# A fused attention and expert-layer kernel: wide code weights, paired evictions, another order of score products, another order table

## The chip, the cores and the metric

The kernel runs on one core of one Trainium2 chip. The metric is the device time of one execution in microseconds. Three runs of the kernel before gave 787.03, 787.33 and 788.19 us; their median, 787.33 us, is the time before.

## The reference

Sixteen heads (2 batches of 8) of 768 tokens and 64 dimensions go through an attention in which a token sees only those keys that fall into its bucket; the result goes through two expert layers without a gate.

```python
q_bits = (einsum('bhsd,dk->bhsk', q, proj) > 0)     # 6 bits a token; k_bits likewise
q_bucket = sum(q_bits * 2 ** arange(6))             # 64 buckets
mask = q_bucket[:, :, :, None] == k_bucket[:, :, None, :]
scores = where(mask, q @ k.T / 8, -1e9)
attn = exp(scores - max); attn = attn / (attn.sum() + 1e-9)
x = (attn @ v) as [1536, 512]
h = x @ w_in;  g = h where h >= 1, 0 where h <= -1, else (h + 1) ** 2 / 4
x = g @ w_out                                       # w_in 512x2048, w_out 2048x512
out = ((x @ w_a) * (x @ w_b)) @ w_out2              # w_a, w_b 512x1536, w_out2 1536x512
```

## The kernel before

Nearly every float32 product is made of three products of an f32r high and low part (high x high, high x low, low x high). A product here is one TensorE matmul of 128 rows, mostly with 384 moving columns (512 in the last layer, 64 or 65 in pv).

**Attention.** For each head, `tk` transposes k (and `kh`, `kl` hold its high and low part), `tq` transposes q into `qt`. `signs` multiplies both with the projection into a bank `kp`, and ScalarE turns that into sign bits `bit` (f16, 103 rows: four groups of six bits, 32 rows apart, with a row of ones). `buckets` multiplies the bits with a constant table of codes: for each of 64 buckets it yields a number whose sign tells whether a token is in that bucket. This goes into a bank `kid`, from where `same` (L588 on ScalarE, L590 on VectorE) writes the upper half of `kl` as 0 or 1, and `f` writes `q2`, which holds a large penalty and the low part of q. So a score tile is four products: `qt` x `kh` and `q2` x `kl`, once for each of the two halves of the keys; each half has a bank of its own (`qk`, L675). A row minimum on VectorE (`mn`, L679) and an exponential on ScalarE (`sm`, L681) follow, then a high and a low part in f16 (`phi`, `plo`), their transposes by DMA on SyncE's queue (`pth`, `ptl`), and the products `pv` with v (L748).

`buckets` has three forms. In batch 0, `i` of 0 or 1 (16 banks, `both`): a product `low` x `qt` (L615) that copies q's low part into rows 64 to 127 of the bank, and then a product of the bits with 64 columns of the code (L616) on top of rows 0 to 63; `f` reads the bank (L621 and L622 on ScalarE, or L624 on VectorE). In batch 0, `i` of 2 (8 banks): a product of 128 code columns (L581), and two reads by `same`, one for each half of the keys. In batch 1 (16 banks): a product of 128 code columns (L581), one read by `same` from rows 64 to 127 and one by `f` (L608 on ScalarE, L610 on VectorE) from rows 0 to 63.

**Expert layers.** `hp` (L1046) is x @ w_in, `acc` (L1258) is g @ w_out; weights come in as 512 KB blocks (`words`), are joined from two 32-bit words and split into high and low parts. The second layer (L1179, L1284) forms x @ w_a and x @ w_b by a seven-product scheme. The first hp needs the attention of all eight heads of the first 384 tokens; from there on attention and expert work are interleaved, and behind the last pv, at some 366 us, there are only expert layers.

**The order.** `Program.add` collects some 3500 operations with the engines that may do each, and its dependencies. Their order, and the engine of each, stands in the table ORDER (L34): a letter for the engine (p TensorE, v VectorE, a ScalarE, g GpSimd, s SyncE's DMA queue) and the step to the operation's number. `schedule` (L225) reads it; each engine works through its own operations in this order. The numbers that `add` gets with an engine are a planner's costs and do nothing at run time; `after` is a dependency that only the order has to respect. Which buffer of a kind an operation gets is set by the order too: `issue` (L241) hands out the one that came free first. Banks of kind `p` (2 of them) and `px` (2, batch 0's early part) hold kid, kp, tk, tq, pv and hp in turn.

Of the kernel before, what the change touches and what calls it, by code (L numbers as in the profile page):

```python
# [39 lines left out]
v-14 a p24 a s-8 v-3 a v142 a-145 v7 g10 v172 p-170 v g18 p-17 v2 a-1 p-8 v g3 p24 a v p-5 a-56 g2 a55 v70 p-102  # L40
p19 v163 g-160 v11 a-25 v12 a182 p-158 a a24 a-53 v54 v-94 v41 a4 p18 s159 s-200 p48 a p-21 v14 v-13 g-2 a18
a221 s-227 g p36 a v p-5 a v p-25 v g-7 g9 a-10 p17 a2 a-1 s-36 a27 s197 a p-192 v p30 v65 p-88 s-40 p31 v33 p2
a-29 g-7 a14 v-3 g2 g15 p-3 v170 v-221 s49 a s-26 a14 g19 v165 a-159 v-11 g-62 p102 a v p-5 a v a-38 p212 p-201
v g11 p-5 a2 s-48 p33 s3 a26 g-20 v v12 p-11 a3 g16 p14 v s-48 v80 g a-66 p7 p27 a67 v a-106 a17 v-5 v-44 v190
s-168 p28 v a20 p15 v g-86 a44 g21 a g12 s-18 v a26 p-25 v p20 v148 s-185 a38 a-20 s97 g-80 p-6 v v-25 p54 a v
a-30 p25 a s-56 g51 a g12 p-16 v a p-15 v150 p-112 a s s-43 a73 g v-15 p-30 a6 s448 a p-438 v-21 p19 v-14 a p123
v-193 s40 p35 a9 p8 p-2 a-1 a33 v-22 v94 v v-109 v7 p26 a-25 g-6 v32 v3 v g-19 s-33 a19 a-4 p15 v p22 a-17 p6 v
s-42 p36 a110 a-93 p9 g-18 a-13 a14 v24 s25 v-24 g-13 v6 s-30 p21 a-11 p42 a5 g v-36 a5 a26 v-49 a19 a12 v-30
p26 p28 a s-59 p27 v-33 v37 v2 g13 p-3 v p25 v s50 a v a-61 v p27 v-26 s-39 v99 a-91 a13 p19 v s-12 a48 v-11
a-41 p22 v v19 a-23 s-43 p25 g17 v7 s-27 a19 v11 p26 v g-2 p6 a p a-37 a79 a-47 s-57 p30 g28 a5 g42 p-27 v-47 v  # L50
v47 a-20 p-15 a v p51 v s23 a v v s-97 a53 a4 s9 a v-13 g-74 p40 a v47 v a-47 v g15 a38 a-52 g p14 a s-39 p57 a
s-4 v20 v7 a-76 s126 g-125 a34 a19 a73 p-61 v p15 a v-47 v v60 a-29 g11 v49 v-73 v-17 p19 p-1 p38 v s-45 a34 s19
a p-46 v27 g13 s-21 p-4 v a v54 p-22 p-15 p-33 s37 p4 s-22 v27 a3 v-2 a-20 g s83 a-57 a28 g v-30 a-19 p16 v s6
p-15 p13 v p-16 v34 a-53 v s68 p-47 a9 a25 p a a-20 g a52 v-15 s-22 p-4 v a v40 v p-53 a p37 a s-116 a79 v35 g20
v-60 a83 g a-51 p-3 s-12 p18 v a v-4 v-28 a p40 a g p-6 a s35 v-44 v-108 p130 v p-27 p-3 p38 g-58 p21 v21 v17 a6
g a-29 v a17 p a-5 a-33 p42 v a-4 v-38 s34 g10 a v18 s-5 a-5 s-18 v19 a-11 v23 p3 a v a-4 a-43 p25 p32 p-21 a22
p-31 s24 v-14 p-13 a14 v-7 p29 a p-35 g-25 p65 p6 v-24 p29 a-15 v13 v-2 g-29 s-4 p48 a-36 v v v-5 v a28 s-19 a15
a11 s-44 a61 p-23 p-24 a34 v-3 a4 s-22 v12 v11 p-24 a-32 v88 s-29 g-18 s7 v-20 p v43 a-51 p42 v a-18 g22 g-16
a-18 v v s140 a-103 g21 s-12 p-13 v s25 p-21 p-44 a45 a-15 v v-14 v10 v5 g-4 a13 p29 a19 a-43 p10 a s19 a-5 g-24
a25 p-11 v p-13 a50 v-26 g27 s-81 a44 a-10 p-3 p9 v s66 p-78 v6 v p-4 s15 p106 a-104 v-162 g p175 a v-14 p22 p2  # L60
a80 v a-107 p25 a-18 p50 v a-37 p-4 v p100 a v a-110 v p16 p20 v-35 g11 a-4 p17 v-16 a165 v s-158 a34 p-49 s40
g-45 p56 s-24 a5 g v-9 s151 a-140 a v v-11 s2 p24 v-97 g a134 v a-66 p22 a p11 v p4 a-63 a37 a-9 v36 v-15 p26
g-37 p59 a-82 v v a43 a-20 v v v19 a a14 p-47 a a84 p-61 a24 s-23 a18 g43 p-49 v p59 a p-28 p-47 p46 a-30 v10 a
v33 v-39 v-4 p59 g-54 p22 s-15 a118 a-105 a35 s-59 p39 v a-55 a58 v-33 s27 v-12 v-39 v a98 s-84 p14 a a-4 a203
# [1335 lines left out]
```

## Time and profile before

| what | us |
|---|---|
| median of three runs | 787.33 |
| the profiled execution | 789.12 |
| its span, first to last instruction | 787.3 |
| TensorE busy | 755.8 (96%) |
| VectorE busy | 665.3 (85%) |
| ScalarE busy | 488.9 (62%) |
| GpSimd busy | 381.7 (48%) |

The profiled execution is not one of the three runs. Busy time is an average over stages with different limits, so it says little here of what a stage is worth. A product of 384 columns stands in the timeline with 0.33 us, but its end is modelled; products overlap, and what one costs is read from the distance of the starts, 0.17 us in a dense stretch. For the same reason TensorE's idle time before a product is some 0.16 us shorter than what the wait costs.

### The profile page before, as it was taken

How to read it: one execution, taken by the hardware profiler on the slowest of the kernel's cores; microseconds unless marked ns; L12 is line 12 of the kernel's file. 1: busy time of each engine (PE TensorE's matmuls, PEld its weight loads, DVE VectorE, ACT ScalarE, POOL GpSimd, SP SyncE). 2: the span in 40 equal slices, each digit the busy share in tenths (PEclk: the TensorE clock that was granted, in tenths of full speed). 3: DMA queues.
4: the chain of work that ended last, by engine and by line, in shares of the span. 5: the costliest groups of instructions: out<-in, count | busy, mean ns of one | idle time of the engine just before them, and what ended most of it. 6: DMA issues, size and time to landing. Idle time of an engine off the chain costs nothing.

```text
span 787.3 us, 14720 instructions
## 1 busy us (share of the span) xinstructions
PE 755.8 (96%) x5532; PEld 696.1 (88%) x5532; DVE 665.3 (85%) x1171; ACT 488.9 (62%) x896; POOL 381.7 (48%) x336
## 2 busy tenths in 40 slices
PE   7888799999999999899999999999999999999998
PEld 4677699998988989889999999999999889999986
DVE  6899899999888998878876856799989897898775
ACT  5889889999988877676554454454434754243232
POOL 1777546546585677563153224354534107534430
PEclk9999999999999999999999999999999999999999
DMA  7999999999799778664012331014432002322011
GB/s 217 194 197 211 234 235 248 235 222 224 165 182 167 133 145 156 122 97 92 2 54 90 102 103 55 27 54 134 134 108 80 14 1 76 99 70 92 1 41 40
DMA packets 202792, 95.50 MB, mean 121 GB/s; under 512 B 165217, under 2 KB 197217, under 8 KB 202721
## 3 DMA queue, kind: packets, MB, share of 16 engines
q1 hardware_dynamic: 202272, 94.39, 52.9%
q8 instruction: 43, 0.70, 0.4%
q14 instruction: 29, 0.23, 0.1%
q10 hardware_dynamic: 448, 0.17, 0.1%
HBM read 53.65 MB, written 3.15 MB: 72 GB/s over the span
## 4 chain that ended last, share of the span: by engine, by line
PE 77%; DVE 11%; ACT 6%; DMA 3%; issue 2%; POOL 1%; SPq 0%; ACTq 0%; POOLq 0%; DVEq 0%
PE hp L1046 15%; PE acc L1258 14%; PE acc L1284 12%; PE mx L1179 12%; PE mz L1179 6%; PE s L675 6%; PE pv L748 5%; PE acc L1179 3%; DVE mn L679 2%; ACT sm L681 2%; PE kp L563 1%; DMA kn<-in_k 1%; PE tq L530 1%; DVE F L948 1%; PE tk L490 1%
## 5 line engine op out<-in xcount | busy, mean ns | idle before, releaser
L376 POOL TENSOR_TENSOR plo<-sm,phi 128x768 f16<-128x768 f32 x58 | 100.7, 1740 | 40.8 <-ACT phi L371 25.7
L679 DVE TENSOR_REDUCE mn<-s 128x1 f32<-128x768 f32 x96 | 91.3, 953 | 15.8 <-PE s L675 15.2
L681 ACT ACTIVATE sm<-s,mn 128x768 f32<-128x768 f32 x96 | 86.3, 900 | 26.2 <-DVE mn L679 25.1
L675 PE MATMUL s<-kh,qt 128*128 128x384 f32 x192 | 70.5, 367 | 4.4 <-ACT sm L681 4.2
L376 POOL TENSOR_TENSOR wlo<-F,whi 128x512 fp32r<-128x512 f32 x41 | 57.0, 1393 | 34.5 <-ACT whi L371 24.1
L1232 ACT ACTIVATE t<-hp,half 128x384 f32<-128x384 f32 x64 | 37.1, 580 | 58.4 <-PE hp L1046 54.4
L675 PE MATMUL s<-kl,q 128*128 128x384 f32 x192 | 65.5, 341 | 2.1 <-ACT q L622 1.0
L376 POOL TENSOR_TENSOR gl<-t,gh 128x384 fp32r<-128x384 f32 x31 | 36.1, 1166 | 49.0 <-ACT gh L371 31.8
L1284 PE MATMUL acc<-whi,gl 128*128 128x512 f32 x144 | 56.7, 394 | 0.0
L1284 PE MATMUL acc<-wlo,gh 128*128 128x512 f32 x144 | 56.7, 393 | 0.0
L1284 PE MATMUL acc<-whi,gh 128*128 128x512 f32 x144 | 56.0, 389 | 0.0
L748 PE MATMUL pv<-vc,pth 128*128 128x65 f16 (+1 forms) x1152 | 51.9, 195 | 2.7 <-DVE q L610 1.7
L1046 PE MATMUL hp<-xsh,whi 128*128 128x384 f32 x152 | 52.0, 342 | 1.6 <-DVE q L610 0.8
L371 ACT ACTIVATE phi<-sm 128x768 f16<-128x768 f32 x63 | 52.8, 841 | 0.7
L1258 PE MATMUL acc<-gh,whi 128*128 128x384 f32 x144 | 52.9, 367 | 0.0
L1241 DVE SCALAR_TENSOR_TENSOR t<-t,hp 128x384 f32<-128x384 f32 x64 | 35.1, 549 | 19.7 <-ACT t L1237 15.8
L748 PEld LDWEIGHTS <-pth 128*128 128x128 f16 x1152 | 42.7, 99 | 9.8 <-issue 9.6
L1046 PE MATMUL hp<-xsh,wlo 128*128 128x384 f32 x152 | 50.9, 335 | 0.0
L1046 PE MATMUL hp<-xsl,whi 128*128 128x384 f32 x152 | 50.9, 335 | 0.0
L1258 PE MATMUL acc<-gh,wlo 128*128 128x384 f32 x144 | 48.5, 337 | 0.0
L1258 PE MATMUL acc<-gl,whi 128*128 128x384 f32 x144 | 48.4, 336 | 0.0
L942 ACT ACTIVATE wab<-stage 128x512 f32<-128x512 f32 x55 | 36.2, 665 | 17.5 <-DMA stage<-in_moe_w_b 3.9
(253 smaller groups left out, 2538.4 us busy)
## 6 DMA issues: line engine op xcount, KB each, us to landing
stage<-in_moe_w_out SPq DMA_DIRECT2D x31, 512.0 KB, 3.9
stage<-in_moe_w_b SPq DMA_DIRECT2D x17, 512.0 KB, 3.7
stage<-in_moe_w_a SPq DMA_DIRECT2D x17, 512.0 KB, 3.6
stage<-in_moe_w_in SPq DMA_DIRECT2D x16, 512.0 KB, 4.7
kn<-in_k SPq DMA_DIRECT2D x16, 192.0 KB, 4.1
out<-ob SPq DMA_DIRECT2D x12, 256.0 KB, 2.1
vn<-in_v SPq DMA_DIRECT2D x4, 384.0 KB, 5.2
vscan<-in_v SPq DMA_DIRECT2D x4, 384.0 KB, 4.8
```

Of the source, the lines that this page charges most:

```text
L371: nc.scalar.activation(dst, src, ACTF.Copy)
L376: (nc.vector if e == "dve" else nc.gpsimd).tensor_tensor(dst, a, b, ALU.subtract)
L675: nc.tensor.matmul(s()[:, i, 0:HC], x()[:, qs], t[i]()[:, 0:HC], start=(n == 0), stop=(n == 1))
L679: add({"dve": c_dve(S)}, lambda e: nc.vector.tensor_reduce(mn(), s()[:, :, 0:HC], AX.XY, ALU.min), r=[s], w=[mn])
L681: o = add({"act": c_act(S, True) + 0.093}, lambda e: nc.scalar.activation(sm().rearrange("p (c n) -> p c n", c=2), s()[:, :, 0:HC], ACTF.E ...
L748: nc.tensor.matmul(o[:, t, 0:D + 1 - i], w()[:, t, c, :], vcs[t]()[:, c, (1 - i) * D:(2 - i) * D + 1 - i], start=(n == 0), stop=(n == 3 * ...
L942: add({"act": 0.556}, lambda e: nc.scalar.activation(ab(), t()[:, :, :, 1].bitcast(F32), ACTF.Prelu, scale=SHIFT, alpha=SIGN), r=[t], w=[a ...
L1046: nc.tensor.matmul(o()[:, 0:TB], a()[:, kk, :], m(), start=(n == 0), stop=(n == 3 * KD - 1))
L1179: nc.tensor.matmul(view()[:, 0:TB], a()[:, sl], m(), start=(start and n == 0), stop=(n == 5), skip_group_check=not start)
L1232: add({"act": 0.465}, lambda e: nc.scalar.activation(t(), o()[:, 0:TB], ACTF.Relu, bias=half, scale=0.5), r=[o], w=[t])
L1258: nc.tensor.matmul(ac()[:, 0:TB], a()[:, d, :], x(), start=(f == 0 and n == 0), stop=(f == F1 - 1 and n == 2))
L1284: nc.tensor.matmul(ac(), a()[:, ts], x().rearrange("p k n -> p (k n)"), start=(f == 0 and n == 0), stop=(f == F2 - 1 and n == 2))
```

## The change

- `qk`: the loops over the half of the keys and over the two terms are swapped, so the four products of a score tile run kh of bank 0, kh of bank 1, kl of bank 0, kl of bank 1.
- `both`: the bits' product comes first, and it takes 128 code columns, of which 64 are zeros, instead of 64; the low part is accumulated on it.
- The code table is 576 columns in nine blocks of 64 instead of 384 columns in three pairs, two blocks being zeros, so that every bits' product takes two neighbouring blocks. For `i` of 2 the two halves of the bank change places.
- `buckets`: of the two reads of a bank the second names the first in `after`.
- ORDER is another table of the same length; the change moves operations on every engine and between engines.

```diff
--- before.py
+++ after.py
@@ -32,128 +32,128 @@
 ORDER = """
-s s2 v3 v p12 a2 v-19 p9 s18 s4 v-28 p3 p8 a-4 v a-4 v p12 s-18 v42 p-29 g30 v-17 p-12 a5 p3 v8 v-6 a-1 p-3 v
-p-5 s276 a v s-284 g p33 a v p a v p-13 v s-10 a p28 a s-26 a v s25 a-20 s12 a31 p-29 v v242 s-23 p-213 p2 s328
...
-a-11 v p11 p7 p-1 v5 v-15 v16 p-4 p7 p-1 p-1 v-4 v a6 v a-15 v p17 v v p-4 p11 a s p-8 a p-5 p7 a s-2 s3
+s3 v3 v p12 a2 s-20 v v3 p6 a v p-5 a v s286 a p-281 p6 a p-6 p v280 s-265 v266 s-270 a p-6 s-20 v42 v v-22 p a
+a p-8 v14 s-20 g p33 p3 a-2 p-9 a12 v-2 s-15 a p24 a p-5 v-3 p10 v-22 a g17 v-2 a g11 p-4 s-34 v v5 p a26 p8 a a
...
+v5 v g-16 p11 p p6 p a v-13 a6 v g7 p-4 p5 v3 v p-2 p9 a s p-8 v s p-6 p7 a s
@@ -345,7 +345,7 @@
     zq_h = const.tile([128, 135], F32R, name="zq_h")
     zq_l = const.tile([128, 135], F32R, name="zq_l")
     zk = const.tile([128, 135], F32R, name="zk")
-    code = const.tile([128, 3, 128], F16, name="code")
+    code = const.tile([128, 576], F16, name="code")
     least = cst[:, 129:130]
     times = cst[:, 130:131]
     thr = cst[0:NR, 128:129]
@@ -578,9 +578,10 @@
         up, dn = slice(0, 64), slice(64, 128)
 
         def mm(e):
-            nc.tensor.matmul(s()[:, 0:HC], code[0:NR, i], bit(), start=True, stop=True)
-
-        def same(c, x):
+            at = 64 * (1 if i == 2 else 3 - 3 * i if b else 5 + 2 * i)
+            nc.tensor.matmul(s()[:, 0:HC], code[0:NR, at:at + 128], bit(), start=True, stop=b > 0 or i == 2)
+
+        def same(c, x, after=()):
             o = d["kl"][c]
 
             def g(e):
@@ -588,11 +589,10 @@
                     nc.scalar.activation(o()[up, 0:HC], s()[x, 0:HC], ACTF.Sign, scale=-1.0)
                 else:
                     nc.vector.tensor_scalar(o()[up, 0:HC], s()[x, 0:HC], 0.0, None, ALU.is_lt)
-            add({"act": c_act(HC, True), "dve": c_dve(HC)}, g, r=[s], w=[o])
+            return add({"act": c_act(HC, True), "dve": c_dve(HC)}, g, r=[s], w=[o], after=after)
         if i == 2:
             add({"pe": 0.18}, mm, r=[bit], w=[s])
-            same(0, up)
-            same(1, dn)
+            same(0, dn, [same(1, up)])
             return
         qt, o = d["q"][c], Buf("q2", [128, HC], F32R)
         d["q2"][c] = o
@@ -601,19 +601,19 @@
             add({"act": c_act(HC), "dve": c_dve(HC, True), "pool": c_pool(HC)},
                 lambda e: copy_on(e, o()[dn], qt()[dn]), r=[qt], w=al[1:])
             add({"pe": 0.18}, mm, r=[bit], w=[s])
-            same(c, dn)
+            first = same(c, dn)
 
             def f(e):
                 if e == "act":
                     nc.scalar.activation(o()[up], s()[up, 0:HC], ACTF.Relu, scale=PEN)
                 else:
                     nc.vector.tensor_scalar(o()[up], s()[up, 0:HC], 0.0, PEN, ALU.max, ALU.mult)
-            add({"act": c_act(HC, True), "dve": c_dve(HC)}, f, r=[s], w=al[:1])
+            add({"act": c_act(HC, True), "dve": c_dve(HC)}, f, r=[s], w=al[:1], after=[first])
             return
 
         def both(e):
-            nc.tensor.matmul(s()[:, 0:HC], low, qt(), start=True, stop=True)
-            nc.tensor.matmul(s()[up, 0:HC], code[0:NR, i, up], bit(), start=False, stop=True, skip_group_check=True)
+            mm(e)
+            nc.tensor.matmul(s()[:, 0:HC], low, qt(), start=False, stop=True)
         add({"pe": 0.35}, both, r=[bit, qt], w=[s] + al)
 
         def f(e):
@@ -670,8 +670,8 @@
 
         def mm(e):
             qs = slice(jj * 128, (jj + 1) * 128)
-            for i in range(2):
-                for n, (x, t) in enumerate(((qt, kh), (q2, kl))):
+            for n, (x, t) in enumerate(((qt, kh), (q2, kl))):
+                for i in range(2):
                     nc.tensor.matmul(s()[:, i, 0:HC], x()[:, qs], t[i]()[:, 0:HC],
                                      start=(n == 0), stop=(n == 1))
         add({"pe": 0.8 if b else 0.86}, mm, r=[qt, (q2, 0), (q2, 1)] + [t[i] for t in (kh, kl) for i in range(2)], w=[s],
@@ -1348,7 +1348,7 @@
         nc.scalar.dma_start(out=cst, in_=consts)
         for i in range(2):
             nc.scalar.dma_start(out=prj[i * D:(i + 1) * D], in_=proj)
-        nc.scalar.dma_start(out=code.rearrange("p i n -> p (i n)"), in_=codes)
+        nc.scalar.dma_start(out=code, in_=codes)
         nc.vector.tensor_copy(idr, idt)
         pr.issue()
 
@@ -1369,11 +1369,12 @@
     c[0:64, 130] = PEN
     bits = np.zeros((32, 64), dtype=np.float16)
     bits[0:nb, 0:64] = 2 * (np.arange(64) >> np.arange(nb)[:, None] & 1) - 1
-    g = np.zeros((128, 3, 128), dtype=np.float16)
-    for i, at, part in ((0, 0, 0), (0, 64, 2), (1, 0, 1), (1, 64, 3), (2, 0, 2), (2, 64, 3)):
-        g[32 * part:32 * part + 32, i, at:at + 64] = bits
-        g[32 * part + nb, i, at:at + 64] = -nb if part > 1 else 1 - nb
-    g = g.reshape(128, 384)
+    g = np.zeros((128, 9, 64), dtype=np.float16)
+    for i, part in enumerate((1, 3, 2, 0, 2, 0, None, 1)):
+        if part is not None:
+            g[32 * part:32 * part + 32, i] = bits
+            g[32 * part + nb, i] = -nb if part > 1 else 1 - nb
+    g = g.reshape(128, 576)
     return c, g
```

## Rows read from the trace of the kernel before

**Rows 1.** Windows: us, busy us (instructions) by engine, clock, DMA share, GB/s.
```profile
10.00:97.00 87.00, 70.99 (x719) 56.55 (x718) 78.05 (x130) 73.82 (x130) 56.86 (x48) 0.96 1.03 209
97.00:160.00 63.00, 63.00 (x565) 59.21 (x566) 60.78 (x100) 56.71 (x104) 33.88 (x29) 1.00 1.06 239
160.00:260.00 100.00, 95.98 (x950) 88.01 (x949) 87.83 (x144) 87.73 (x157) 59.48 (x48) 1.00 0.94 190
260.00:380.00 120.00, 115.33 (x1114) 107.89 (x1111) 102.46 (x169) 85.39 (x146) 73.04 (x61) 1.00 0.64 116
380.00:788.00 408.00, 402.57 (x2166) 380.84 (x2164) 330.76 (x612) 181.83 (x356) 157.63 (x146) 1.00 0.21 66
```

**Rows 2.** TensorE's timeline, 287 us: start us, us, engine, line, operation, tiles.
```profile
287.49 0.34 PE L1258 MATMUL acc<-gh,wlo 128*128 128x384 f32 x1
287.67 0.34 PE L581 MATMUL kid<-bit,code 103*128 103x384 f16 x1
287.71 0.48 PE L675 MATMUL s<-kh,qt 128*128 128x384 f32 x1
288.03 0.34 PE L675 MATMUL s<-kl,q 128*128 128x384 f32 x1
288.20 0.33 PE L675 MATMUL s<-kh,qt 128*128 128x384 f32 x1
288.37 0.34 PE L675 MATMUL s<-kl,q 128*128 128x384 f32 x1
```

**Rows 3.** Chain that ended last, pieces: start us, us, what.
```profile
96.82 3.22 PE hp L1046 x17
```

**Rows 4.** Timeline of TensorE at 111 us.
```profile
111.47 0.34 PE L615 MATMUL kid<-qt,eye 128*128 128x384 f32 x1
111.74 0.35 PE L616 MATMUL kid<-bit,code 103*64 103x384 f16 x1
112.02 0.44 PE L1258 MATMUL acc<-gh,whi 128*128 128x384 f32 x1
...
112.47 0.35 PE L1258 MATMUL acc<-gh,wlo 128*128 128x384 f32 x1
```

**Rows 5.** Timeline of TensorE at 147 us.
```profile
146.86 0.42 PE L615 MATMUL kid<-qt,eye 128*128 128x384 f32 x1
147.21 0.35 PE L616 MATMUL kid<-bit,code 103*64 103x384 f16 x1
...
147.95 0.34 PE L1258 MATMUL acc<-gh,wlo 128*128 128x384 f32 x1
```

**Rows 6.** Lines L616, L581: weight loads, ns min/median/max.
```profile
L616 PEld LDWEIGHTS <-code x16: 106/106/106, 10.2 to 157.7; 103*64 103x64 f16 x16
...
L581 PEld LDWEIGHTS <-code x24: 95/98/100, 9.5 to 336.1; 103*128 103x128 f16 x24
```

**Rows 7.** TensorE's waits, 0 to 97 us: total us, times, longest.
```profile
PE kid L616 <- ACT bit L568: 0.6, 1, 0.6
```

**Rows 8.** Page, costliest groups: busy us, mean ns; idle us.
```profile
L748 PEld LDWEIGHTS <-pth 128*128 128x128 f16 x1152 | 42.7, 99 | 9.8 <-issue 9.6
```

**Rows 9.** Waits of ScalarE and VectorE, 97 to 380 us: total us, times, longest.
```profile
ACT kl L588 <- DVE q L610: 3.2, 2, 2.0
...
DVE q L610 <- ACT kl L588: 3.4, 3, 1.7
```

**Rows 10.** TensorE's waits, 97 to 380 us.
```profile
PE pv L748 <- DVE q L610: 1.7, 2, 0.9
PE s L675 <- DVE kl L590: 0.9, 1, 0.9
...
PE hp L1046 <- DVE q L610: 0.8, 1, 0.8
```

**Rows 11.** Line L610: duration in ns min/median/max.
```profile
L610 DVE TENSOR_SCALAR q<-kid x9: 509/548/550, 175.4 to 310.3; 64x384 fp32r<-64x384 f32 x9
```

**Rows 12.** GpSimd's groups, 0 to 97 us: busy us, mean ns; idle us.
```profile
L373 POOL CAST phi<-sm 128x768 f16<-128x768 f32 x7 | 6.5, 924 | 7.8 <-ACT sm L681 7.8
```

More of the change, by code (lines that the diff above doesn't have):

```diff
@@ L40 @@
[L40 to L64, printed above, removed]
@@ new lines @@
+g13 v-6 g2 v141 v-187 a51 g14 a-16 g19 g10 a199 p-174 a a78 v-46 v-1 p-73 p11 a p8 v-19 v42 a-22 a v194 v-233
+p55 v p-26 v s-4 v26 g s-33 v117 a-119 a15 p v104 a-103 p-12 a8 a154 p-143 p25 a v-12 g-11 v-2 v57 v86 g-85 s-80
+v19 p22 v a-15 a-4 g22 s-6 a129 p-120 a s-24 g19 g13 a-17 p-12 a15 g-23 g40 p4 v v p-4 a p-9 v a v-27 v p69 a
+p-16 a v81 p-92 p13 a-9 s62 p-59 a v-7 a s-50 p35 s40 v-15 s-28 p154 s-153 p45 v-21 p19 s-11 a40 v-43 v17 a36
+g-64 g13 s2 a-3 g43 p-38 s92 v27 v-71 a-49 a15 s17 a-22 p8 a v-5 a6 p-4 v71 v34 g-90 s2 p12 a-32 g21 a34 g v-52
@@ new lines @@
+p11 v18 p5 a v-2 v-21 s124 g-110 a-13 a14 g12 p-16 v p-6 v p25 v a-20 g17 g7 p-13 a41 p-31 p21 a5 v-35 a v-18
+v27 a p11 s-19 a10 v18 p6 a p-32 p37 p5 a52 v-59 s-9 v-9 a a25 p p18 s-64 v38 a49 v10 v-76 a55 g a-53 v-56 p57
+v73 s-76 a21 v-3 g2 g7 v16 v v22 v-41 a-6 a11 p26 v p4 a44 s-104 p30 g28 a-33 a32 v4 p a s30 a s-67 v4 v p12
+v-37 v38 v a38 p13 v p-20 v a v15 v p-49 g12 v22 s40 a-73 a74 s-94 a21 v-16 g-24 g96 s24 s-47 a21 p-4 v a g-67
+p32 a21 v-37 s109 a-108 p34 a p20 v17 v a-57 v21 v14 s-19 p44 a s8 s-26 a-42 a92 v-108 v55 v-38 a v91 p-46 g-6
@@ new lines @@
+g-83 g8 s s a-12 v58 g-45 g17 g-108 p83 a p80 a-50 s366 a-290 a-32 a-29 v36 v p-81 v p6 v v v36 v29 p-56 a-16
+a22 g16 s2 a-23 p v p49 a v p69 g-35 p-76 a p112 a-121 g-106 p226 a-110 p-6 p114 v-113 v7 p3 a-12 a3 v10 a v29
+p39 a v p-57 v a-10 s-7 s5 a17 s5 g6 v41 a a27 p-84 v a p126 a a p-97 a g-77 p48 g-2 v82 v-27 p100 p2 a-5 v-149
+a g4 a21 a40 v59 p-119 g-4 s2 v146 p-128 v p6 a p123 p-2 a-25 v p-84 s-8 v32 v-60 v61 a-44 v139 a-126 v83 g-95
+v9 g-84 g171 p-90 v a a11 a14 p107 s-129 p130 p-128 a v23 v-6 v108 a-107 p111 p-115 v s19 p94 v-127 a115 a-100
@@ new lines @@
+g20 v-3 p85 a p-82 a83 s-85 g13 g-46 v115 a-79 v83 p-91 v p-11 a a a10 g17 s5 g-1 v69 v v7 g p a a p-110 v v
+p114 p p-96 v a g9 p a v77 v p7 a g p-3 a-4 p-88 v a s3 v7 v75 a-74 s5 a209 p-131 g-79 s2 v70 a19 a-11 p-88 v a
+p99 a-8 a-82 v89 p-2 v-9 v a p-86 v g88 v-2 a-85 v13 a82 p-6 g-75 p-9 p83 s-61 g-1 s2 a68 a-90 p4 v p79 p18 a-96
+g17 a71 v-3 v v-161 v162 a7 a3 p-86 p7 v-6 a86 v a-86 a8 s4 g70 p-3 p-1 v-96 v94 v-69 v4 s2 p84 a a p-22 p14
+a-85 v109 v v-133 p97 v9 v11 g-10 p13 v p-10 v11 a-18 g p4 p p16 v v p-102 a92 p17 g-16 g-118 a111 g a-86 p96 v
```

193 lines of the change are left out of this document (99 added, 94 removed).

## The prediction

> **What bounds the kernel now.** I read the windows by stage first. From 380 us to the end TensorE is busy 402.57 of 408 us [rows 1]. That is more than half of the span, and no order of the work can shorten it: products of 384 columns follow each other every 0.17 us there, as from 288.03 to 288.37 in [rows 2]. From 97 to 160 us TensorE is busy all the time too [rows 1]. What can move is TensorE's idle time before 97 us (87.00 - 70.99 = 16.0 us between 10 and 97) and between 160 and 380 us (4.0 + 4.7 = 8.7 us), and what a product costs beyond 0.17 us. Before 97 us there is only attention to run, for the first product of the expert layers (hp) starts at 96.82 [rows 3]; VectorE is busy 78 and ScalarE 74 of 87 us there, the DMA share is 1.03, and the granted clock is 0.96 on average [rows 1]. That stage is a mesh of limits, and a saving on TensorE reaches the end only in part. Behind 97 us the expert layers fill TensorE, and what one of its products or waits costs there comes off the end in full.
>
> **The bits' product: what is removed.** Sixteen banks (`both`, batch 0) get a low-part product (L615), and on top of it the bits' product whose f16 weights are 64 columns wide (L616). In [rows 4] the pair starts at 111.47, two more products follow from 112.02 on, and the next starts at 112.47: 1.00 us for four products. In [rows 2] the 128-column bits' product (L581) stands between f32r products: from 287.49 to 288.20 four products start, the bits' one among them, 0.71 us. The 64-column form thus costs 1.00 - 0.71 = 0.29 us more than the 128-column one with f32r work on both sides, which is how it will stand after the change (bits, then low part). Where a transpose or a pv product stands ahead, as at 147 us, the four take 147.95 - 146.86 = 1.09 us [rows 5], 0.38 more than 0.71. The interval from L615 to L616 tells the two forms apart (0.27 as in [rows 4], 0.35 or more as in [rows 5]). Behind 97 us there are five such banks, three of the first and two of the second form: 3 x 0.29 + 2 x 0.38 = 1.6 us, all on the path. Before 97 us there are eleven, four of the first form and seven of the second: 4 x 0.29 + 7 x 0.38 = 3.8 us, of which I count half, 1.9 us (bounds 0 and 3.8), since TensorE waits in that stage for engines that are not shortened.
>
> The wider weights are no cost by the trace: the load of 103x128 takes 98 ns, that of 103x64 106 ns [rows 6]. The Trainium skill ("TensorE: Matmul & The Clock Gate", LDWEIGHTS) speaks against this edit: a load's time goes with its column count, P / 1.2 ns. By that rule 64 more columns are 53 ns, 16 x 53 ns = 0.9 us lost, and the sum would end at 781.4 instead of 780.5 us. The trace disagrees, 98 against 106 ns, so the measurement decides.
>
> **Bits first.** The wait for the bits now stands ahead of both products, where the low part used to run before it; everything on TensorE's queue is behind it. One wait of this kind is to be seen before 97 us, 0.6 us [rows 7], and it would grow by one product, 0.17 us. If each of the sixteen waited it would be 16 x 0.17 = 2.8 us; I take nothing for the one, as it lies in the half that I don't count.
>
> **Scores alternate their banks.** The four products of a score tile stay; only kl of bank 0 and kh of bank 1 change places. In [rows 2] 288.03 to 288.20 changes the bank, 288.20 to 288.37 does not, and both steps are 0.17 us: no gain and no loss. The row minimum waits for all four either way. Equal weights now stand side by side; the pv products already use each pth block twice in a row, and a load is still issued for each of the 1152 [rows 8]. The bound on the gain is 0.173 - 0.160 us (384 columns at 2.4 GHz) for 192 products, 2.5 us; I take 0. A wait for kl or q2 now finds two products ahead of it instead of one, 0.17 us less a time; one such wait is in [rows 10] (s for L590), and I leave it out.
>
> **Two evictions in succession.** A bucket bank is read twice, for kl and for q2. When the two reads are on different engines they don't overlap in the trace, they wait for each other: between 97 and 380 us ScalarE stands 3.2 us for VectorE's q2, VectorE 3.4 us for ScalarE's kl [rows 9]. The program keeps them apart already, so the new `after` adds no wait on the chip; it makes the order table follow it. By the new table 15 of the 16 such banks of batch 1 have both reads on one engine, by the old one 5; of batch 0's eight pairs of kl, 7 against 3. TensorE's waits that end with such a read (L610, L590) sum to 1.7 + 0.9 + 0.8 = 3.4 us behind 97 us [rows 10]. I take two thirds, 2.3 us (bounds 0 and 3.4): a bank's second read, 0.5 us [rows 11], still has to end before pv or hp can have the bank. The Trainium skill ("PSUM — Partial Sum Buffer", PSUM bank collisions) says that two engines may read different quadrants of one bank at once, and kl's and q2's reads do lie in different ones; by that rule succession would give up an overlap of 0.5 us in each of 16 banks, and this term could be a loss. No row here shows such an overlap; the waits in [rows 9] show the opposite of it in this program.
>
> **The new order table.** All products stay, TensorE's list is reordered, 610 of 3514 operations change engine (net: 12 more on GpSimd, 5 fewer on VectorE, 7 fewer on ScalarE). Of the other waits between 160 and 380 us 8.7 - 3.4 = 5.3 us are left. What I can read from the tables alone is how much TensorE work stands between the last product into a bank and the next product that takes that bank over. Between 97 and 380 us the old table has 19 places with less than 1 us there (a product's 0.33 us and one eviction of 0.5 us fill most of that), the new one 13; in one of these there is none at all (an hp right behind a tq), a stall of 0.33 + 0.5 - 0.17 = 0.7 us. So 5.3 x 6/19 = 1.7 us, less 0.7: 1.0 us gained. Bounds: all 5.3 gained, or 3 us lost, as new waits can cost what half of the old ones do.
>
> Before 97 us: ahead of the first hp the new table has GpSimd do 12 phi casts instead of 7, 5 x 0.92 = 4.6 us more [rows 12], VectorE none instead of 6; SyncE issues 54 transfers instead of 56 (one weight block of 512 KB and one K head of 192 KB fewer: 0.7 MB at 209 GB/s [rows 1] are 3.3 us). One for, one against; I take 0, with bounds of 3.3 us gained and 4.6 us lost. The code table grows from 96 to 147 KB, on ScalarE's queue among the first transfers, as before; all later work is behind it there only for the issue, which stays one instruction: 0.
>
> **The sum.** 1.6 + 1.9 + 2.3 + 1.0 = 6.8 us. The profiled execution took 789.12 us, 1.8 beyond its span of 787.3; after: 782.3. The median of the runs is 787.33, also 1.8 below the profiled one, and I carry that distance over: 780.5 us.
>
> **Rivals.** First, the larger gain: all 3.8 us of the early banks and the 3.3 us of the lighter DMA queue count, and all 3.4 us of the evictions. For it: the DMA share of 1.03. Against it: VectorE is at nine tenths. 787.3 - (1.6 + 3.8 + 3.3 + 3.4 + 1.0) = 774.2 us. Second, absorbed: the early stage gives nothing and new waits take the place of the old ones; only the five banks behind 97 us count: 785.7 us. Third, the change does not do what it says: the bits' product costs its 0.29 us through its f16 type, not its 64 columns, and the terms of 1.6 and 1.9 vanish: 784.0 us. Against it stands L581, f16 too, in [rows 2]. The Trainium skill ("TensorEngine Tiling (Array Packing)", Key Properties) has a rule for the width: a change of the tiling mode drains the engine. Fourth, slower: GpSimd becomes the bound before 97 us. Its phi casts stand ahead of the plo differences on the same queue, and these ahead of the transposes and pv; the five added casts lie on that chain and put the first hp 4.6 us later, while the waits behind 97 us are only replaced: 787.3 + 4.6 - 1.6 = 790.3 us. It decides once GpSimd has less than 4.6 us of slack in the stretch that leads to the last pv before the first hp; over the whole stage it has 87 - 57 = 30 us [rows 1], which speaks against it.
>
> **Chances.** Forecast 0.55, larger gain 0.12, no gain from the width 0.09, absorbed 0.14, slower 0.10. The bound of 0.2% is 1.6 us, about what a measurement of this kernel can tell from no change. 785.7 lies at that bound; a fifth of its chance goes to faster. Faster 0.55 + 0.12 + 0.09 + 0.03 = 0.79, same 0.11, slower 0.10. With every term at its good end, the early transfers left out, the time is 787.3 - (1.6 + 3.8 + 3.4 + 5.3) = 773.2 us; with every one at its bad end 787.3 - 1.6 + 3 + 4.6 = 793.3. The range of eight in ten goes from the first to a little above the time before, and leaves out the slower rival: 773.0 to 788.0 us.
>
> **What would show it.** Right: L616 is gone; bits, low part and their neighbours take 0.7 us for four; the first hp starts near 95 us; TensorE's idle time between 160 and 380 us is near 5.5 us; from 380 us on nothing is gained. Wrong: a step of 0.27 us or more at the bits' product, a first hp behind 97 us, or new waits of TensorE for GpSimd's plo or the transposes.

## The result, and the profile after

The changed kernel takes 781.82 us (median of four runs, 780.03 to 782.55) against 787.41 us for the kernel before in the same series: a ratio of 0.9916, 95% interval 0.989 to 0.9943. The forecast was 780.5 us. The profiled execution took 782.20 us with a span of 780.4.

The windows of the changed kernel, by the stages of [rows 1] (us; busy us and instructions of TensorE, its weight loads, VectorE, ScalarE, GpSimd; granted clock; DMA share; GB/s):

```profile
10.00:97.00 87.00, 71.96 (x729) 59.10 (x727) 79.85 (x132) 72.74 (x123) 60.74 (x53) 0.94 1.04 209
97.00:160.00 63.00, 61.22 (x555) 57.35 (x553) 59.69 (x100) 56.89 (x104) 30.34 (x22) 1.00 1.03 234
160.00:260.00 100.00, 98.59 (x989) 92.92 (x989) 92.07 (x158) 91.40 (x164) 58.64 (x51) 1.00 0.93 194
260.00:380.00 120.00, 118.15 (x1123) 111.82 (x1122) 99.28 (x164) 85.89 (x151) 75.30 (x64) 1.00 0.65 115
380.00:788.00 408.00, 395.61 (x2119) 375.22 (x2117) 334.08 (x595) 175.89 (x345) 168.93 (x155) 1.00 0.21 67
```

(The last window ends behind the kernel.) TensorE's idle time between 160 and 380 us is 1.41 + 1.85 = 3.3 us; it was 8.7 [rows 1]. Between 97 and 160 us it idles 1.8 us, where it idled none. Its waits from 97 to 380 us (total us, times, longest) answer [rows 10]; the wait for a second read of a bucket bank is left once, 1.4 us, and two new ones, for sm and for qt, lie before 160 us:

```profile
PE pv L748 <- DVE q L610: 1.4, 1, 1.4
PE s L675 <- ACT sm L681: 1.1, 1, 1.1
PE kid L582 <- DVE t L1241: 0.8, 1, 0.8
PE hp L1046 <- ACT qt L542: 0.6, 1, 0.6
```

The bits' product of batch 0 in a dense stretch of the changed kernel, TensorE's timeline (it answers [rows 4]): from 125.02 to 125.73 four products start, 0.71 us. The loads of its 128 columns have a median of 98 ns (min/median/max; all banks), as in [rows 6].

```profile
125.02 0.34 PE L582 MATMUL kid<-bit,code 103*128 103x384 f16 x1
125.06 0.47 PE L616 MATMUL kid<-qt,eye 128*128 128x384 f32 x1
125.37 0.34 PE L1258 MATMUL acc<-gh,whi 128*128 128x384 f32 x1
125.55 0.34 PE L1258 MATMUL acc<-gl,whi 128*128 128x384 f32 x1
125.73 0.33 PE L1258 MATMUL acc<-gh,wlo 128*128 128x384 f32 x1
```
```profile
L582 PEld LDWEIGHTS <-code x40: 95/98/146, 10.3 to 329.2; 103*128 103x128 f16 x40
```

The first hp starts a microsecond earlier than in [rows 3]:

```profile
95.84 0.42 PE L1046 MATMUL hp<-xsh,whi 128*128 128x384 f32 x1 [0.52 <-DVE xsl L376]
```

The span falls into three parts by two starts on TensorE's timeline: the first hp, and the last pv product, behind which only expert layers run. All kernels of this study by these marks, in us (the clock is the mean granted one from 10 to 97 us, in which stage it fell to its lower level, 1.2 GHz, for one to three short stretches; behind 97 us it is 1.00):

| kernel | median, runs | ratio, 95% | first hp, clock | first hp to last pv | last pv to end |
|---|---|---|---|---|---|
| before | 787.41, 4 | | 96.82, 0.96 | 268.60 | 421.89 |
| after | 781.82, 4 | 0.9916, 0.989 to 0.9943 | 95.84, 0.94 | 262.11 | 422.46 |
| e1_narrow_bits | 784.07, 5 | 0.9957, 0.9944 to 0.997 | 96.97, 0.94 | 261.58 | 422.45 |
| e2_old_scores | 782.55, 6 | 0.9934, 0.992 to 0.9948 | 94.47, 0.98 | 262.06 | 422.44 |
| e3_wide_alone | 789.42, 11 | 1.0017, 1.0005 to 1.0029 | 95.18, 0.98 | 267.81 | 423.37 |
| e4_table_alone | 782.56, 5 | 0.994, 0.9928 to 0.9952 | 98.49, 0.92 | 263.34 | 420.33 |
| f1_before_pad | 789.74, 12 | 1.0021, 1.0009 to 1.0033 | 95.24, 0.98 | 268.68 | 423.40 |
| f2_after_moved | 780.37, 4 | 0.99, 0.9883 to 0.9917 | 98.05, 0.93 | 260.75 | 420.33 |
| f3_split_reads | 786.70, 12 | 0.9981, 0.9968 to 0.9994 | 96.39, 0.96 | 266.16 | 422.44 |
| f4_after | 781.99, 6 | 0.9926, 0.9909 to 0.9943 | 95.40, 0.98 | 261.81 | 422.42 |
| g1_wlo_pool | 777.54, 4 | 0.9866, 0.9846 to 0.9886 | 95.69, 0.94 | 259.51 | 420.28 |
| g2_low_first | 779.95, 5 | 0.9895, 0.9874 to 0.9916 | 95.61, 0.96 | 262.22 | 420.32 |
| g3_narrow_bits | 782.51, 6 | 0.9935, 0.9915 to 0.9955 | 97.75, 0.94 | 262.83 | 420.32 |
| g4_wlo_pool_32 | 780.48, 5 | 0.991, 0.989 to 0.993 | 96.82, 0.96 | 260.74 | 422.25 |

The e, f and g kernels stand beside runs of the kernel before of their own, with medians of 788.01, 788.31 and 788.11 us. A difference of two rows carries both intervals, together some 2 us. Where it is smaller than that, the marks are read beside it; they come from one profiled execution of each kernel. f4 is the changed kernel once more, beside the other f kernels:

> The changed kernel again, on the same chip as the three others, as the reference for them: 6.0 us under the kernel before (ratio 0.992), 384-column spacing 175.45 ns behind the last pv product, TensorE idle in 160 to 380 us about 3.3 us.

Measured: 781.99 us, 6.3 under the kernel before, spacing (explained below) 175.44 ns, TensorE idle for 3.2 us from 160 to 380 us.

### The profile page after: what moved, and what is told of

The parts are those of the page before. It is cut to its first block, busy times and chain, and to the rows that moved or that the text cites. A ratio compares the mean times of both kernels' runs of the same rounds, so it can differ in the third digit from the quotient of the medians.

```text
span 780.4 us, 14723 instructions
## 1 busy us (share of the span) xinstructions
PE 752.7 (96%) x5532; PEld 700.5 (90%) x5532; DVE 669.7 (86%) x1166; ACT 486.4 (62%) x891; POOL 394.2 (51%) x348
## 4 chain that ended last, share of the span: by engine, by line
PE 81%; DVE 11%; issue 3%; ACT 2%; POOL 2%; DMA 1%; ACTq 0%; DVEq 0%; POOLq 0%
PE hp L1046 15%; PE acc L1258 15%; PE acc L1284 12%; PE mx L1179 12%; PE s L675 7%; PE mz L1179 6%; PE pv L748 5%; PE acc L1179 3%; DVE mn L679 2%; PE kp L563 2%; PE tq L530 1%; DVE wlo L376 1%; PE tk L490 1%; DVE plo L376 1%; DMA ptl<-plo 1%
## 5 line engine op out<-in xcount | busy, mean ns | idle before, releaser
L376 POOL TENSOR_TENSOR plo<-sm,phi 128x768 f16<-128x768 f32 x60 | 105.1, 1757 | 38.0 <-ACT phi L371 32.1
L376 POOL TENSOR_TENSOR wlo<-F,whi 128x512 fp32r<-128x512 f32 x34 | 47.7, 1405 | 33.2 <-ACT whi L371 15.5
L675 PE MATMUL s<-kh,qt 128*128 128x384 f32 x192 | 55.7, 372 | 4.1 <-ACT sm L681 3.9
L376 POOL TENSOR_TENSOR gl<-t,gh 128x384 fp32r<-128x384 f32 x30 | 34.1, 1140 | 49.3 <-ACT gh L371 32.6
L371 ACT ACTIVATE whi<-F 128x512 fp32r<-128x512 f32 x71 | 43.8, 624 | 14.8 <-PE acc L1284 11.0
L675 PE MATMUL s<-kl,q 128*128 128x384 f32 x192 | 50.1, 342 | 0.4 <-ACT q L622 0.4
L376 DVE TENSOR_TENSOR wlo<-F,whi 128x512 fp32r<-128x512 f32 x56 | 46.4, 830 | 2.1 <-ACT whi L371 1.7
```

Of the source, the lines that this page charges most:

```text
L371: nc.scalar.activation(dst, src, ACTF.Copy)
L376: (nc.vector if e == "dve" else nc.gpsimd).tensor_tensor(dst, a, b, ALU.subtract)
L675: nc.tensor.matmul(s()[:, i, 0:HC], x()[:, qs], t[i]()[:, 0:HC], start=(n == 0), stop=(n == 1))
```

## The experiments

**Parts of the change alone.** e1 keeps everything of the change but the width and the order of the bits' product; e2 all but the order of the scores; e3 makes only the width, the order bits first and the larger code table; e4 takes only the new table ORDER.

e1, in `both` of the changed kernel:

```diff
-            mm(e)
-            nc.tensor.matmul(s()[:, 0:HC], low, qt(), start=False, stop=True)
+            at = 64 * (5 + 2 * i)
+            nc.tensor.matmul(s()[:, 0:HC], low, qt(), start=True, stop=True)
+            nc.tensor.matmul(s()[up, 0:HC], code[0:NR, at:at + 64], bit(), start=False, stop=True, skip_group_check=True)
```

> The changed kernel with the sixteen bits' products of batch 0 as they were: low part first, then the bits' product of 64 code columns on top. All else, the order table too, as changed. Theory (the width of the product costs 0.29 to 0.38 us each, five of them in the dense stretch, half of the eleven early ones on the path): 3.5 us slower than the changed kernel, 785.3 us; 0.27 us and more between L616 and its neighbours again. Rival (the f16 type costs, or the stage absorbs it): within 1 us of the changed kernel, 781 to 783 us.

Measured: 784.07 us, some 2.1 us slower than the changed kernel (f4; by the ratios 0.0031 x 788 = 2.4). In its dense stretch the four products take 1.00 us again, 126.12 to 127.12 in TensorE's timeline:

```profile
126.12 0.34 PE L616 MATMUL kid<-qt,eye 128*128 128x384 f32 x1
126.39 0.35 PE L617 MATMUL kid<-bit,code 103*64 103x384 f16 x1
126.67 0.44 PE L1259 MATMUL acc<-gh,whi 128*128 128x384 f32 x1
126.95 0.34 PE L1259 MATMUL acc<-gl,whi 128*128 128x384 f32 x1
127.12 0.34 PE L1259 MATMUL acc<-gh,wlo 128*128 128x384 f32 x1
```

So the price of the narrow form is its width, as forecast, 0.29 us in a dense stretch. (e1 takes back the order of the two as well; in g2 below the low part comes first with 128 code columns behind it, and the four take 0.71 us, 124.74 to 125.45.) The first hp comes 1.1 us later than in the changed kernel at the same mean clock. From there to the last pv e1 is no slower, 261.58 us against 261.81 in f4: f4 has TensorE's wait of kid for t, 0.8 us, near 174 us, and e1 has not.

e2, in `qk` of the changed kernel:

```diff
-            for n, (x, t) in enumerate(((qt, kh), (q2, kl))):
-                for i in range(2):
+            for i in range(2):
+                for n, (x, t) in enumerate(((qt, kh), (q2, kl))):
```

> The changed kernel with the four products of a score tile in the old order (both terms of one bank, then the other). Theory (every step is 0.17 us, bank changed or not): no difference, within 0.8 us of the changed kernel. Rival (a wait for q2 or kl is covered by one product more, 0.17 us for each of some tens of waits, or equal weights side by side save 0.013 us for each of 192 products): 2 to 3 us slower.

Measured: 782.55 us, 0.6 above f4, inside both intervals; from the first hp on the two agree to 0.3 us. The order of the scores is worth nothing that shows here.

e3, in the kernel before:

```diff
-    code = const.tile([128, 3, 128], F16, name="code")
+    code = const.tile([128, 576], F16, name="code")
...
-            nc.tensor.matmul(s()[:, 0:HC], low, qt(), start=True, stop=True)
-            nc.tensor.matmul(s()[up, 0:HC], code[0:NR, i, up], bit(), start=False, stop=True, skip_group_check=True)
+            mm(e)
+            nc.tensor.matmul(s()[:, 0:HC], low, qt(), start=False, stop=True)
```

> The kernel before with the wide bits' product ahead of the low part alone (code table of nine blocks for it); old order table, old order of the scores. Theory: 1.6 us from the five dense places and half of 3.8 us from the early ones, 787.4 - 3.5 = 783.9 us. Rival (only the dense places count): 785.8 us. Rival (the whole gain is the width's): 782 us.

Measured: 789.42 us, 1.4 us slower than the kernel before beside it (interval 0.4 to 2.3). That contradicted the forecast of 3.5 us for this part, and the marks say where: 0.8 us gained up to the last pv, 1.5 us lost behind it, where no bits' product runs. The first hp is no help: its mean clock differs from that of [rows 1].

e4, in the kernel before:

```diff
-ORDER = """ (the old table) """
+ORDER = """ (the new table) """
```

> The kernel before with the new order table alone: narrow bits' product on top of the low part, old order of the scores. Theory (two terms of 2.3 and 1.0 us behind 160 us): 787.4 - 3.3 = 784.1 us, with TensorE's idle time between 160 and 380 us near 3.3 us, as in the changed kernel, instead of 8.7. Rival (the table only fits the changed products and is no gain without them): 787 us or more.

Measured: 782.56 us, 5.4 us under the kernel before beside it by the medians (interval by the ratio 3.8 to 5.7): most of the whole gain. TensorE's idle time from 160 to 380 us is 1.41 + 2.22 = 3.6 us without any other edit, and the waits for sm (1.1 us) and for qt (0.6) between 97 and 160 us are there too: both come from the table. Its windows:

```profile
160.00:260.00 100.00, 98.59 (x967) 92.24 (x964) 92.34 (x157) 91.02 (x163) 59.94 (x51) 1.00 0.92 195
260.00:380.00 120.00, 117.78 (x1151) 111.45 (x1151) 99.48 (x167) 85.88 (x151) 76.19 (x65) 1.00 0.67 117
```

**Where the width's gain went: the place of the tiles.** Behind the last pv all kernels of one table run the same program, yet e3 runs 1.5 us slower there than the kernel before, and the changed kernel 2.1 us slower than e4. (The new table orders the work there in another way, and better: the kernel before has 23 steps over 0.2 us behind a 384-column product there, 7.9 us in all, e4 has 15, 5.5 us in all.) In the timeline the mean distance of the starts of 384-column products behind the last pv is 174.05 ns in the kernel before and 173.90 in e4, but 175.45 in the changed kernel, e1, e2 and e3 (about 1755 products, 2.5 us); 512-column ones go the other way, 230.1 to 229.1 ns (430 products, 0.4 us). The slow group has the code table of 576 columns. It lies among the constants at the left end of SBUF, and its 384 more bytes per partition move every tile behind it: dense activations, weights, x and g. Tiles that are handed out from the right end stay, among them the high parts wkh of the first layer's kept weights; of their low parts wkl all but the first lie at the left. f1 moves the tiles and does nothing else:

```diff
     code = const.tile([128, 3, 128], F16, name="code")
+    pad = const.tile([128, 192], F16, name="pad")
```

> The kernel before with 384 bytes per partition of SBUF allocated behind the code table and never touched; no instruction is added or changed. Theory A (the place of the left-hand SBUF tiles sets the pace of the expert layers): every tile from the dense activations to the expert weights moves from address 480 to 352 modulo 512, as in the changed kernel, so the mean start-to-start time of the 384-column products behind the last pv product goes from 174.05 to about 175.45 ns (1757 of them, +2.5 us), that of the 512-column ones from 230.1 to about 229.1 ns (430, -0.4 us), and the run is 2.1 us slower than the kernel before (near 790.1 on a chip where that takes 788.0); attention is as before. Rival B (the slower pace came with the new products or the new transfers, not with the place): spacing 174.05 ns and the time of the kernel before, within 0.3 us.

Measured: 789.74 us, 1.4 us slower than the kernel before beside it (interval 0.7 to 2.6), spacing 175.47 and 228.96 ns, and 1.5 us more behind the last pv. An allocation that nothing reads costs this. Of the 2.1 us that were expected the slower steps cost 2.2; 0.7 us comes back from shorter waits behind the last pv (7.2 us in steps over 0.2 us instead of 7.9). f2 takes the tables away from the left end, so that the tiles lie 1536 bytes lower than in the kernel before:

```diff
-    eye = const.tile([128, 192], F32R, name="eye")
+    eye = P["tab"].tile([128, 192], F32R, name="eye")
...
-    code = const.tile([128, 576], F16, name="code")
+    code = P["tab"].tile([128, 576], F16, name="code")
...
-    scopes["att"] = open_pools(ATT, side="right")
+    scopes["att"] = open_pools(ATT + ("tab",), side="right")     # ahead of the constants
```

> The changed kernel with its identity table and its code table (768 and 1152 bytes per partition) moved from the left-hand constants into the attention's right-hand scope; the left-hand tiles lie 1920 bytes lower, at 480 modulo 512 as in the kernel before, the attention's own tiles lie where they were. No instruction changes. Theory A (place sets the pace): 384-column spacing behind the last pv product back to about 174.05 ns, 512-column to 230.1, and 2.1 us less than the changed kernel beside it (near 780.2 where the kernel before takes 788.0). Rival B: spacing stays at 175.45 ns and the time within 0.3 us of the changed kernel's.

Measured: 780.37 us, 1.6 under f4, spacing 173.95 and 230.09 ns, 2.1 us less behind the last pv. Theory A holds both ways. The products with wkh show it, from 430 to 770 us (busy us, mean ns of one; kernel before, f1, f4, f2 in turn): 336 ns, then 341, 340, and 336 again.

```profile
L1258 PE MATMUL acc<-gl,wkh 128*128 128x384 f32 x68 | 22.8, 336 | 0.4 <-DVE gl L376 0.4
```
```profile
L1259 PE MATMUL acc<-gl,wkh 128*128 128x384 f32 x68 | 23.2, 341 | 0.4 <-DVE gl L377 0.4
```
```profile
L1258 PE MATMUL acc<-gl,wkh 128*128 128x384 f32 x58 | 19.7, 340 | 0.2 <-DVE gl L376 0.2
```
```profile
L1259 PE MATMUL acc<-gl,wkh 128*128 128x384 f32 x58 | 19.5, 336 | 0.2 <-DVE gl L377 0.2
```

g4 puts the tiles 64 bytes beyond a good place, on top of g1 (below):

```diff
     code = P["tab"].tile([128, 576], F16, name="code")
+    pad = const.tile([128, 32], F16, name="pad")
```

> g1 with 64 bytes per partition of unused SBUF in the constants: the left-hand tiles lie at 32 modulo 512, 64 bytes beyond their place in the kernel before (480), the right-hand ones at 480 as ever. Theory A1 (the 128 bytes that the changed kernel moved them the other way cost 1.4 ns a product; what counts is the distance from the right-hand tiles, in either direction): 384-column spacing behind the last pv product between 174.1 and 175.4 ns, and 0.2 to 2 us slower than g1. Theory A2 (only some places cost): 174.0 ns and the time of g1, within 0.3 us.

Measured: 780.48 us, 2.9 us slower than g1, 2.0 of it behind the last pv; spacing 175.03 and 228.85 ns. Theory A1's sign is right, its bound of 2 us too small; 0.8 us of the rest is TensorE's wait of kid for t, which g1 has not. 64 bytes away from the place in g1 cost about as much as 384 bytes away from that in the kernel before, and the 1536 bytes between these two places cost nothing. Why a product's pace depends on it is open.

**Two evictions in succession.** f3 gives twelve reads of batch 1's bucket banks back to the engines of the old table; order and all else stay. Eight go from ScalarE to VectorE, four the other way, and 5 of the 16 banks are left with both reads on one engine instead of 15. Each flip is a letter in ORDER:

```diff
-a (operations 900, 1026, 1149, 1253, 1349, 1446, 1539, 1543)   v (1257, 1450, 1538, 1636)
+v                                                              a
```

> The changed kernel with the engines of its twelve differing bucket-bank evictions of batch 1 set as in the old order table, so that a bank's two evictions lie on two engines again; order and all else as in the changed kernel. The prediction's theory (the table's gain from 160 us on comes from a bank's evictions in succession on one engine): TensorE's idle time in 160 to 380 us goes from 3.3 up to about 6 us, and the run is about 2.3 us slower than the changed kernel (near 784.3 where the kernel before takes 788.0). Rival (the gain is in the order in which the table issues the work, and the engines of these evictions matter little): idle near 3.3 us and the time within 0.5 us of the changed kernel's.

Measured: 786.70 us, 4.7 us slower than f4, and 4.4 us more from the first hp to the last pv. TensorE's idle time from 160 to 380 us is 2.94 + 3.51 = 6.5 us:

```profile
160.00:260.00 100.00, 97.06 (x967) 90.53 (x967) 91.08 (x157) 88.22 (x159) 58.34 (x50) 1.00 0.92 190
260.00:380.00 120.00, 116.49 (x1126) 110.22 (x1123) 97.34 (x164) 84.11 (x147) 75.50 (x65) 1.00 0.65 116
```

The reads themselves, by line from 160 to 380 us (busy us, mean ns; idle us of their engine ahead of them), in f3 and in the changed kernel:

```profile
L614 DVE TENSOR_SCALAR q<-kid 64x384 fp32r<-64x384 f32 x9 | 4.9, 547 | 1.4 <-ACT kl L593 1.2
...
L612 ACT ACTIVATE q<-kid 64x384 fp32r<-64x384 f32 x7 | 3.4, 484 | 3.9 <-DVE kl L595 3.9
```
```profile
L608 ACT ACTIVATE q<-kid 64x384 fp32r<-64x384 f32 x11 | 5.3, 485 | 0.2
...
L610 DVE TENSOR_SCALAR q<-kid 64x384 fp32r<-64x384 f32 x5 | 2.8, 550 | 0.1
```

With the reads split ScalarE stands 3.9 us for VectorE's read and VectorE 1.2 us for ScalarE's, as in [rows 9]; in succession the second read starts at once. The theory's direction is right and its size is half of what it is. TensorE's waits in f3 from 97 to 380 us:

```profile
PE s L679 <- ACT sm L685: 2.3, 5, 1.1
PE pv L752 <- ACT q L612: 1.2, 1, 1.2
PE kid L586 <- DMA stage<-in_moe_w_out: 1.1, 1, 1.1
...
PE tq L534 <- DVE tl L377: 0.5, 1, 0.5
PE kid L586 <- DVE q L614: 0.5, 1, 0.5
```

Three of them end with a bank's read, 1.2 + 1.1 + 0.5 = 2.8 us, against 1.4 us in the changed kernel. The 1.1 us stand there under a transfer into stage, a tile that a bits' product doesn't use; the timeline shows what the product waited for. It starts 0.05 us behind the end of q on ScalarE, and q had stood 1.97 us for VectorE's read of the same bank:

```profile
268.42 0.56 DVE L595 TENSOR_SCALAR kl<-kid 64x384 fp32r<-64x384 f32 x1
...
269.02 0.48 ACT L612 ACTIVATE q<-kid 64x384 fp32r<-64x384 f32 x1 [1.97 <-DVE kl L595]
...
269.55 0.32 PE L586 MATMUL kid<-bit,code 103*128 103x384 f16 x1 [1.14 <-DMA stage<-in_moe_w_out]
```

Most of the other half of the added waiting ends with work of the same two engines: the waits for sm are 2.3 us instead of 1.1, and the one for tl (0.5 us) is new. That this work is late because a read ahead of it was late fits its place in the queues; wait by wait it was not traced.

**The order and the width, with the tiles in place.** g2 and g3 change `both` of f2.

```diff
-            mm(e)
-            nc.tensor.matmul(s()[:, 0:HC], low, qt(), start=False, stop=True)
+            at = 64 * (5 + 2 * i)
+            nc.tensor.matmul(s()[:, 0:HC], low, qt(), start=True, stop=False)
+            nc.tensor.matmul(s()[:, 0:HC], code[0:NR, at:at + 128], bit(), start=False, stop=True)
```

> f2 with the low part of a bucket bank of batch 0 ahead of the bits' product again, both 128 columns wide. The prediction put the order of the two at nothing: within 0.3 us of f2, 780.4 where the kernel before takes 788.3. Rival (the order matters, since a bank whose bits come late keeps TensorE waiting with the low part not yet done): bits' waits of TensorE change and the run is 0.5 to 1 us faster than f2 with the low part first.

Measured: 779.95 us, 0.4 under f2 and inside its interval: the order of the two is worth nothing that shows. g3 has e1's edit instead:

> f2 with the bits' product of batch 0 in its old form, 64 columns wide on top of the low part, and nothing else changed; the place of the tiles and the order table stay. The prediction's theory (sixteen wide products save 0.29 to 0.38 us each, those that TensorE works through without a pause all of it, the early ones half): 2.0 to 3.5 us slower than f2, near 783. Rival (the early products' saving is lost in TensorE's waits there, and five late ones alone count): 0.9 to 1.6 us slower, near 781.6.

Measured: 782.51 us, 2.1 us slower than f2, at the forecast theory's lower end, and the same as e1 against f4. From the first hp to the last pv it takes 0.6 us more than g2 (both profiles have TensorE's wait of kid for t, 0.8 us, which f2's lacks, so g2 is the fairer one to compare); ahead of the first hp it takes 2.1 us more than g2, at a lower mean clock.

**The new wait between 97 and 160 us.** TensorE waits 1.1 us for sm, which waits for a row minimum on VectorE (107.89). Ahead of that minimum VectorE makes a wlo, in f2's timeline:

```profile
105.33 1.30 DVE L377 TENSOR_TENSOR wlo<-F,whi 128x512 fp32r<-128x512 f32 x1
106.56 0.94 DVE L377 TENSOR_TENSOR plo<-sm,phi 128x768 f16<-128x768 f32 x1
107.42 0.54 DVE L377 TENSOR_TENSOR gl<-t,gh 128x384 fp32r<-128x384 f32 x1
107.89 0.94 DVE L680 TENSOR_REDUCE mn<-s 128x1 f32<-128x768 f32 x1
```

g1 gives that one operation to GpSimd, one letter of ORDER:

```diff
-v (operation 487, wlo)
+g
```

> The version with the tables on the right-hand side (f2), with one operation on another engine: the low part of a dense weight that VectorE makes at 105.3 us (128x512, 1.30 us) goes to GpSimd, which makes the same in 1.30 to 1.73 us and stands idle there. In f2 it lies on VectorE ahead of a row minimum and of the softmax's read that TensorE waits for at 110.7 us (1.1 us). Theory C (what the new order table lost between 97 and 160 us is VectorE's queue ahead of that read): the wait falls below 0.3 us and the run is about 0.9 us faster than f2 (near 779.5 where the kernel before takes 788.3). Rival D (the wait is a transfer's or an activation's, or TensorE only waits elsewhere): within 0.3 us of f2, 780.4.

Measured: 777.54 us, 2.8 us under f2 and the fastest kernel of this study, 1.3% under the kernel before. The wait for sm is gone; the waits and the window of f2, then of g1, from 97 to 160 us:

```profile
PE s L676 <- ACT sm L682: 1.1, 1, 1.1
PE hp L1047 <- ACT qt L543: 0.6, 1, 0.6
PE hp L1047 <- DVE xsl L377: 0.5, 1, 0.5
```
```profile
PE hp L1051 <- ACT qt L547: 0.6, 1, 0.6
```
```profile
97.00:160.00 63.00, 60.63 (x550) 56.76 (x550) 59.76 (x100) 55.97 (x102) 29.89 (x23) 1.00 1.04 228
```
```profile
97.00:160.00 63.00, 62.28 (x563) 58.80 (x563) 60.03 (x103) 58.54 (x107) 32.08 (x23) 1.00 1.07 244
```

Theory C holds for the place and the wait, but it expected 0.9 us. The profiles show 1.2 us between the first hp and the last pv; the rest is ahead of the first hp (98.05 against 95.69 in the two profiled executions, which are 3.6 us apart), where the table's entries are the same, and no run tells what it is.

## Why the prediction was right, and where it was not

The time was right to 1.3 us, the sign too, and the mechanisms in the main; the split was not. The parts as measured: table 5.4 (e4), width 2.1 (e1, g3), scores and order of the bits 0 (e2, g2), the tiles' place -1.6 (f2): 5.9 us, against 5.6 and 6.3 us measured as a whole (after, f4). The forecast sum was 6.8. That it came so near is in part luck: the table gave 2.1 us more than its two terms of 2.3 and 1.0, the width 1.4 less than forecast, and the tiles' place took 1.6 that had no term.

- **The bits' product.** The price was right: four products take 0.71 us, not 1.00, and L616 with 64 columns is gone. Put at 1.6 + 1.9 = 3.5 us, it is worth 2.1. Of the 1.6 for the five banks behind 97 us 0.6 us is left in g3 against g2, 0.9 in e3 against f1, and nothing in e1 against f4, where one wait of 0.8 us covers it. The step that failed is that a product's cost there "comes off the end in full". With the timelines of two kernels side by side, product by product, the five banks do cost 1.3 us more in g3 than in g2 and 1.5 us more in f1 than in e3. But 0.7 us of it comes back in either pair, 0.1 to 0.3 us at a time, at an s, a kp or an hp, in the old table as in the new. I read that as the faster kernel coming early to work that isn't ready: up to 0.13 us a time shows there as its TensorE's idle time. Of the 1.9 for the eleven early ones e1 shows 1.1 at the first hp, and in the old table (e3 against f1, same clock) 0.1: "half" was a choice, and how much counts depends on the table. In the old table the whole width is worth 0.3 us by the medians (e3 against f1), less than they can tell from nothing.
- **The third rival**, the f16 type and not the width, is out by e1.
- **The wider loads and the larger table.** A load of 128 columns takes 98 ns, as forecast; one of 64 took 106 [rows 6]. The rule of the Trainium skill ("TensorE: Matmul & The Clock Gate", LDWEIGHTS), by which more columns take longer to load, is not what these rows show. But the larger table moved the expert layers' tiles and cost 1.6 us. The step that failed is "the code table grows from 96 to 147 KB ...: 0": it asked for the transfer alone and not for what lies behind the tile in SBUF. "From 380 us on nothing is gained" is right by cancellation: the table gains 1.6 us behind the last pv (e4 against the kernel before), which had no term either, and the place loses 2.1 (f4 against f2).
- **Two evictions in succession** were put at 2.3 us with an upper bound of 3.4 and are worth 4.7 (f3). The step that failed is the bound: it summed TensorE's waits that stand under a bank's read [rows 10], and f3 shows one that stands under another name. The two reading engines' own standstill, 3.2 + 3.4 us [rows 9], held as a bound here: f3 has 3.9 + 1.2 us of it, the changed kernel none, and the loss is 4.7. f3 doesn't fully tell the succession from the balance, since VectorE has four more reads in it and ScalarE four fewer: from the first hp to the last pv VectorE is busy 236.0 us against 234.2 in f4, ScalarE 219.6 against 221.5. The 1.8 us more on VectorE are less than half of the 4.4 that this part takes longer. The rule that was weighed against this edit, that two engines may read different quadrants of a bank at once (the Trainium skill, "PSUM — Partial Sum Buffer", PSUM bank collisions), would have made f3 the faster one. f3 does not try that rule, since this program lets the second read start only behind the first, as the 1.97 us above show; with that, splitting the reads costs 4.7 us.
- **The rest of the new table** was put at 1.0 us; 5.4 - 4.7 leaves 0.7. By the marks it is a larger gain, less a loss: from the first hp to the last pv e4 gains 5.3 us, 0.9 more than f3 takes back, and behind the last pv 1.6 more; ahead of the first hp it loses 1.7 us at a lower mean clock (0.92 against 0.96), and no run tells how much of that is the table's. The 0.9 us are what is left after the waits for sm and qt before 160 us that the forecast didn't see: it took that stage as full, and its 0.7 us for a single tight bank is not where they are. g1 shows that one of them was the engine of one operation. TensorE's idle time of 3.3 us instead of 5.5 comes with the mis-sized term above.
- **Ahead of 97 us** the first hp at 95.84 is near the 95 that were named. The fourth rival, GpSimd's casts, didn't come: GpSimd makes 13 phi casts up to 97 us, 11.3 us by the line below, and TensorE waits for VectorE and ScalarE (its three largest sums follow).

```profile
L373 POOL CAST phi<-sm 128x768 f16<-128x768 f32 x13 | 11.3, 870 | 6.6 <-ACT sm L681 6.3
```
```profile
PE s L675 <- ACT sm L681: 2.8, 4, 1.1
PE kp L563 <- DVE kl L376: 2.4, 2, 1.7
PE tq L530 <- DVE xsl L376: 1.8, 1, 1.8
```

## What to carry to other kernels

When two engines drain one bank in turn, bound what keeping it on one engine is worth by the time that these engines stand for each other, not only by the waits of TensorE that name the read: a late read can come out in TensorE's waits under another name. When a change makes a tile larger, look up which tiles it moves, and measure an empty allocation of the same size before the change is judged: here it hid three quarters of what the wider product gained with the new table, and all of it with the old one. A stage that is full before a new order need not be full after it; look there first for what the order lost. And a stage in which TensorE looks full can still give back a part of a saving at its next wait.
